# Linear attention with a gated MLP: output weights kept by head group, packed through DRAM for later tiles, and a reordered middle

## The chip, the cores and the metric

One core of a Trainium2 chip runs the whole program. The time is that of the device in microseconds (us), from launch to the last store; the kernel before takes 190.83 us in the median of three runs (190.46 to 190.95). A core has a matrix engine (TensorE, in the profile PE, its weight loads PEld), a vector engine (VectorE, DVE), an engine for activation functions (ScalarE, ACT), a general one (GpSimd, POOL) and a queue engine (SyncE, SP) that here only issues transfers. Each works through its own list of instructions in order and waits on semaphores for the others.

## The reference

A pre-norm block on 2048 rows of 448 columns in bfloat16: linear attention with 16 heads of 28 columns, and a gated MLP of width 1792. Cut to what matters:

```python
phi = lambda t: jnp.where(t > 0, t + 1, jnp.exp(t)) + 1e-6
pq, pk = phi(q), phi(k)
kv = jnp.einsum("bhsd,bhse->bhde", pk, v)
z = jnp.einsum("bhsd->bhd", pk)
num = jnp.einsum("bhqd,bhde->bhqe", pq, kv)
den = jnp.einsum("bhqd,bhd->bhq", pq, z)[..., None] + 1e-6
h = x + (num / den).reshape(B, S, D) @ wo
h2 = h + (gelu(g) * u) @ w_down        # g, u = layernorm(h) @ w_gate, w_up
```

## The kernel before

**Tiles.** The 2048 rows are 16 tiles of 128 rows, or 8 pairs (pair p holds tiles 2p and 2p + 1). Stage A1 normalises each tile, projects it to keys and queries (tasks `k_t`, `q_t`: four matmuls of 448 columns each), applies phi, and sums pk with the normalised x over all tiles (`pt`). From that sum `kv` makes the per-head products; the masked copy of it, `kvm`, multiplied by the output weights, gives `w2`: the attention's output is then pq, divided by its denominator, times w2.

**Stage A2**, one pair at a time (`a2_pair`): `cq` and `aq` finish phi of the queries; `t1` multiplies by z, `dr` sums over the 28 columns of a head, `de` adds epsilon on ScalarE, `rd` takes the reciprocal and `pn` scales pq (into `pqn`). This is transposed, for pair 0 on TensorE (`tro`, evicted by `evo`), for the others by a DMA transpose (`oT_p`, line 605). `out` multiplies by w2, `hr` adds x, `bnst2` and `bnag2` are the statistics of the second layer norm, POOL or ScalarE make its factor, `nh` scales, `wrap` or `wr64` repeats columns, and `trh` (pair 0) or a DMA transpose `hT_t` turns the tile for the MLP. A name ending in P works on a whole pair at once.

**Stage B**: `gu2_v` (chunks of two tiles, v = 0 to 13) and `gu4_v` (four tiles) compute gate and up products into two PSUM banks each, `ge` the gelu on ScalarE, `hm` the product on VectorE, each in two halves of 256 columns; `downA_p` and `downB_p` multiply by w_down for a pair, `fo` adds, `do` stores. wd_sb, the down weights, is loaded by one transfer, `dwd` (line 609), before which `downA_0` can't start.

**How w2 is held before.** Its 448 rows stand in four blocks of 128 rows (the last one overlapping), so that pairs 1 to 7 can run as two matmuls at once, one on the upper 64 rows of the array for one tile and one on the lower 64 for the other (`outA_p`, `outB_p`, lines 627 and 628; seven such steps in all, and `outB_p` waits for `outA_p`, because both add into the same banks). To get the blocks, `kvm` is written with wide zero gaps and `w2` takes seven matmuls (line 547). The other arrangement of the rows, shifted by 64, is made by two transfers from SBUF to SBUF, `dws0` and `dws1`.

**Order.** The order on each engine is written out by hand: `ORDERS` holds one list of task numbers per engine, a task's number being its place in the program. From the dependences `plan` works out which semaphore waits are needed. `HOLD` names, for a task with several waits, the one to issue first (lines 198 to 201).

The orders in the middle, by name (before):

```
PE   pt3_13 pt3_14 pt3_15 q_5 q_4 kv q_7 q_8 w2_2 w2_0 w2_1 q_9 w2_3 tro_1 tro_0 q_6 out1_1 out1_0 q_10 q_11 q_13 q_12
     q_14 q_15 trh_1 trh_0 outA_1 outB_1 gu2_0 gu2_1 outA_2 gu2_2 gu2_3 outB_2 gu2_4 gu2_5 outA_3 gu2_6 outB_3 downA_0 gu2_8 gu2_7
DVE  aq_3 cq_1 evpD_3 z0 aq_1 t1d_0 dr_0 evpD_2 rd_0 dr_1 dr_2 kvm rd_2 kvd dr_3 rd_1 pn_0 rd_3 pn_1 evwD_1 cqP_2 evwD_3
     pn_2 pn_3 aqP_2 hr_1 hr_0 bnst2_1 bnst2_0 bnag2_1 bnag2_0 drP_2 nhD_1 nhD_0 rdP_2 wr64_1 wr64_0 pnP_2 cqP_3 aqP_3 evhD_1
     hr_2 hr_3 bnst2_2 drP_3 hm1_0 hm0_0 bnst2_3 hm0_1 rdP_3 hm1_1 pnP_3
SP   dwg0 dwu0 dwg1 dwu1 dws0 dws1 oT_1 oT_2 dwd oT_3 hT_3 hT_2 hT_4 oT_4 hT_5 hT_7 hT_6 oT_5
```

Of the kernel before, what the change touches and what calls it, by code (L numbers as in the profile page):

```python
# [228 lines left out]
def bass_sequential_preLN__linear_attn_block__glu_gated_geglu__prompt_kernel(  # L229
# [19 lines left out]
    with es:  # L249
# [281 lines left out]
        op("dve", lambda e: e.tensor_tensor(kvz[:, 0:5 * D].rearrange("p (g c) -> p g c", g=NG)[:, :, 0:GW].rearrange("p g (h f) -> p g h f", h=4),  # L531
                                            ps[0:GW, BK_KV, 0:D].rearrange("p (g h f) -> p g h f", g=NG, h=4),
                                            mask[:, :].unsqueeze(1).unsqueeze(3).to_broadcast([GW, NG, 4, DH]), ALU.mult),
           [b_ps[BK_KV], b_mask, b_kvm], [b_kvm], "kvm")
        b_kvd = _Buf("kvd")
        op("dve", lambda e: e.tensor_copy(kvz[:, 4 * D:4 * D + 64], kvz[:, 4 * D - 64:4 * D]), [b_kvm], [b_kvd], "kvd")

        def kvc(g, c):
            o = g * D + c * 128 if c < 3 else 4 * D - 64
            return kvz[:, o:o + 128]  # L540

        for c in range(4):
            def fw2(e, c=c):
                gs = (c, c + 1) if c < 3 else (3,)
                ins = None
                for g in gs:
                    ins = e.matmul(ps[:, BK_W2[c], 0:D], kvc(g, c), wo_sb[:, g, :], start=(g == gs[0]), stop=(g == gs[-1]))  # L547
                return ins
            G.add("pe", fw2, r=[b_kvm, b_wo] + ([b_kvd] if c == 3 else []), w=[b_ps[BK_W2[c]]], name="w2_%d" % c)
            if c % 2 == 0:  # L550
                op("act", lambda e, c=c: e.activation(w2[:, c, :], ps[:, BK_W2[c], 0:D], AF.Identity), [b_ps[BK_W2[c]]], [b_w2[c]], "evwA_%d" % c)
            else:
                op("dve", lambda e, c=c: e.tensor_copy(w2[:, c, :], ps[:, BK_W2[c], 0:D]), [b_ps[BK_W2[c]]], [b_w2[c]], "evwD_%d" % c)
# [4 lines left out]
        def a2_pair(p):
            a = 2 * p
            i2 = p % 2  # L560
            pst = D if p else 512
            if p < 2:
# [7 lines left out]
                for t in (a, a + 1):  # L570
                    n, i = t % 2, t % 4
                    op("dve", lambda e, n=n, i=i: e.tensor_reduce(den[:, i, :], t1[:, n, :].rearrange("p (h d) -> p h d", h=H), AX.X, ALU.add),  # L572
                       [b_t1[n]], [b_den[i]], "dr_%d" % t)
                    op("act", lambda e, i=i: e.activation(den[:, i, :], den[:, i, :], AF.Identity, bias=eps_d[:, 0:1]), [b_den[i], b_epsd], [b_den[i]], "deA_%d" % t)
                    op("dve", lambda e, i=i: e.reciprocal(rd[:, i, :], den[:, i, :]), [b_den[i]], [b_rd[i]], "rd_%d" % t)
                    op("dve", lambda e, t=t, n=n, i=i, i2=i2: e.tensor_tensor(
                        pqn[:, i2, n * pst:n * pst + D].rearrange("p (h d) -> p h d", h=H), pq[:, t, :].rearrange("p (h d) -> p h d", h=H),
                        rd[:, i, :].unsqueeze(2).to_broadcast([128, H, DH]), ALU.mult),
                       [b_pq[t], b_rd[i]], [b_pqn[i2][n]], "pn_%d" % t)
# [243 lines left out]
```

## Time and profile before

| | |
|---|---|
| median of 3 runs | 190.83 us (190.46 to 190.95) |
| span of the profiled execution | 188.3 us |
| TensorE matmul busy | 184.3 us (98%) |
| VectorE busy | 129.3 us (69%) |
| ScalarE busy | 76.5 us (41%) |
| POOL busy | 50.0 us (27%) |

The profile is one execution. Its views: the page (busy shares, the chain of work that ended last, groups of instructions), groups by line and shape, the timeline, which gives the start and the duration of each instruction, and windows, which give busy time for a stretch. A group's row has the line, the engine, the operation, what is written from what, the shapes, the count, then busy us and mean ns, then idle time before. Task names are not in the profile; they follow from the order of each engine's instructions.

### The profile page before, as it was taken

The page shows a single profiled execution, that of the slowest core. Times are in us where ns is not written, and L with a number is a line of the kernel's source. Part 1 is how long each engine was busy: PE and PEld are TensorE (multiplying, and loading weights), DVE is VectorE, ACT ScalarE, POOL GpSimd, SP SyncE. Part 2 cuts the span into 40 slices and gives each one's busy share as a digit, 9 for nine tenths or more (in the row PEclk, how much of TensorE's full clock was granted, in tenths as well). Part 3 has the DMA queues.
Part 4 walks back from the last instruction along what each step waited for, and adds up shares of the span by engine and source line. Part 5 has one row for each costly group of instructions (what it writes and reads, how often), then busy time and mean ns, then how long its engine had stood idle before and what let it go on. Part 6 is the DMA issues. An engine that isn't in the chain of part 4 may idle for free.

```text
span 188.3 us, 4459 instructions
## 1 busy us (share of the span) xinstructions
PE 184.3 (98%) x1813; PEld 109.2 (58%) x1813; DVE 129.3 (69%) x330; ACT 76.5 (41%) x220; POOL 50.0 (27%) x91
## 2 busy tenths in 40 slices
PE   7999999999999999999999999999999999999994
PEld 7545555555688788965554555555545545454554
DVE  4999959999899998786796762562645244335432
ACT  3878752799963231432234222321242222224100
POOL 6067910704505686033614000206100000000000
PEclk9999999999999999999999999999999999999999
DMA  5996458999393526820005720000096000002024
GB/s 169 387 231 88 96 104 194 218 222 174 65 320 64 95 52 116 84 52 0 0 3 98 144 54 0 0 3 2 3 135 111 3 0 24 3 0 98 3 79 140
DMA packets 35076, 17.11 MB, mean 91 GB/s; under 512 B 26864, under 2 KB 33648, under 8 KB 35056
## 3 DMA queue, kind: packets, MB, share of 16 engines
q1 hardware_dynamic: 34432, 16.32, 41.1%
q10 hardware_dynamic: 624, 0.52, 0.8%
q8 instruction: 14, 0.23, 0.5%
q14 instruction: 6, 0.05, 0.1%
HBM read 8.26 MB, written 1.84 MB: 54 GB/s over the span
## 4 chain that ended last, share of the span: by engine, by line
PE 94%; DVE 3%; DMA 1%; issue 0%
PE ps L733 38%; PE ps L697 19%; PE ps L469 12%; PE ps L731 9%; PE ps L488 6%; PE ps L627 3%; PE ps L678 3%; PE ps L628 2%; DMA x_sb<-in_A_x_dram 1%; DVE st L413 1%; PE ps L617 1%; PE ps L547 1%; PE ps L527 1%; PE ps L443 0%; PE ps L654 0%; DVE den L572 0%
## 5 line engine op out<-in xcount | busy, mean ns | idle before, releaser
L733 PE MATMUL ps<-hnT,wgu_sb 64*128 64x512 bf16 (+1 forms) x490 | 88.8, 333 | 0.0
L731 PE MATMUL ps<-hnT,wgu_sb 64*128 64x512 bf16 (+1 forms) x490 | 88.6, 333 | 0.0
L751 ACT ACTIVATE gl<-ps 128x256 bf16<-128x256 f32 x112 | 36.6, 383 | 85.3 <-PE ps L731 84.4
L753 DVE TENSOR_TENSOR hh<-ps,gl 128x256 bf16<-128x256 f32 x112 | 42.1, 416 | 41.4 <-ACT gl L751 41.3
L733 PEld LDWEIGHTS ps<-hnT,wgu_sb 64*128 64x128 bf16 x490 | 45.2, 94 | 32.9 <-DVE hh L753 3.4
L731 PEld LDWEIGHTS ps<-hnT,wgu_sb 64*128 64x128 bf16 x490 | 45.4, 94 | 2.5
L697 PE MATMUL ps<-wd_sb,hh 64*128 64x448 bf16 x392 | 41.5, 349 | 0.0
L697 PEld LDWEIGHTS ps<-wd_sb,hh 64*128 64x128 bf16 x392 | 23.2, 94 | 14.5
L469 PE MATMUL ps<-wqk_sb,xnT 128*128 128x448 bf16 x128 | 27.4, 353 | 0.0
L413 DVE BATCH_NORM_STATS2 st<-x_sb 128x6 f32<-128x448 bf16 x32 | 19.2, 612 | 1.8 <-DMA x_sb<-in_A_x_dram 1.7
L585 POOL TENSOR_TENSOR t<-pq,zbc 128x448 f32<-128x448 bf16 x12 | 12.3, 1042 | 23.7 <-DVE pq L583 22.0
L469 PEld LDWEIGHTS ps<-wqk_sb,xnT 128*128 128x128 bf16 x128 | 11.9, 98 | 11.4 <-DVE pk L482 0.8
L488 PE MATMUL ps<-pk,xnn 128*128 128x448 bf16 x64 | 13.9, 352 | 0.0
L627 PE MATMUL ps<-w,pqnT 64*128 64x448 bf16 x49 | 11.5, 349 | 0.1
L425 POOL TENSOR_SCALAR ln<-mv 128x2 f32<-128x2 f32 x7 | 2.0, 291 | 35.2 <-DVE mv L414 35.0
L480 ACT ACTIVATE e<-ps 128x448 bf16<-128x448 f32 x16 | 8.5, 539 | 5.6 <-PE ps L469 5.5
L628 PE MATMUL ps<-pt_sb,pqnT 64*128 64x448 bf16 x42 | 10.2, 350 | 0.0
L633 DVE TENSOR_TENSOR x_sb<-ps,x_sb 128x448 bf16<-128x448 f32 x16 | 9.6, 616 | 0.7 <-PE ps L628 0.6
L662 POOL TENSOR_SCALAR hn<-x_sb,nm,rs 128x448 bf16<-128x448 bf16 x14 | 9.9, 719 | 0.4
L482 DVE SCALAR_TENSOR_TENSOR pk<-ps,e 128x448 bf16<-128x448 f32 x16 | 9.8, 617 | 0.1
L488 PEld LDWEIGHTS ps<-pk,xnn 128*128 128x128 bf16 x64 | 6.3, 98 | 5.9 <-DVE pk L482 0.3
L453 POOL TENSOR_SCALAR xnn<-x_sb,nm,rs 128x448 bf16<-128x448 bf16 x12 | 8.9, 744 | 2.2 <-ACT rs L422 1.9
(85 smaller groups left out, 160.5 us busy)
## 6 DMA issues: line engine op xcount, KB each, us to landing
out_dram<-x_sb SPq DMA_DIRECT2D x15, 112.0 KB, 1.8
wd_sb<-in_B_w_down_dram SPq DMA_DIRECT2D x1, 1568.0 KB, 8.4
x_sb<-in_A_x_dram SPq DMA_DIRECT2D x3, 448.0 KB, 5.9
wgu_sb<-in_B_w_gate_dram SPq DMA_DIRECT2D x1, 896.0 KB, 12.1
wgu_sb<-in_B_w_up_dram SPq DMA_DIRECT2D x1, 896.0 KB, 16.5
wgu_sb<-in_B_w_gate_dram SPq DMA_DIRECT2D x1, 672.0 KB, 6.1
wgu_sb<-in_B_w_up_dram SPq DMA_DIRECT2D x1, 672.0 KB, 8.5
wo_sb<-in_A_wo_dram SPq DMA_DIRECT2D x1, 392.0 KB, 7.5
```

What stands on the lines that cost most here:

```text
L413: op("dve", lambda e: e.bn_stats(st[:, t, :], src_ap), [b_src], [b_st[t]], "bnst%s_%d" % (tag, t))
L469: ins = e.matmul(ps[:, bk, 0:D], xnT[:, t, k, :], wqk_sb[:, k, c0:c0 + D], start=(k == 0), stop=(k == 3))
L488: ins = e.matmul(ps[:, BK_PT[c], 0:D], xnn[:, t % XN_R, c * 128:(c + 1) * 128], pk[:, ip, :], start=(t == 0), stop=(t == T - 1))
L585: op("pool", lambda e, n=n: e.tensor_tensor(t1[:, n, :], pq[:, a + n, :], zbc[:, :], ALU.mult), [b_pq[a + n]] + b_z, [b_t1[n]], "t1p_%d" % ...
L627: e.matmul(ps[:, BK_OUT[0], 0:D], pqnT[ra, i2, sg // 2, :], w2[ra, sg // 2, :], start=(sg == 0), stop=(sg == 5))
L628: ins = e.matmul(ps[:, BK_OUT[1], 0:D], pqnT[rb, i2, 3 + (sg + 1) // 2, :], (w2 if sg == 6 else w2s)[rb, sg // 2, :], start=(sg == 0), sto ...
L662: op("pool", lambda e, t=t, sh=sh: e.tensor_scalar(hn[:, sh, 0:D], x_sb[:, t, :], nm2[:, t:t + 1], rs2[:, t:t + 1], ALU.add, ALU.mult), [b ...
L697: ins = e.matmul(ps[:, bko[half][n], 0:D], hh[rows, j, sl[n]], wd_sb[rows, j, :], start=(j == 0 and (half == 0 or p == 6)), stop=(j == NJ ...
L731: first = e.matmul(psG[:, jj * N:(jj + 1) * N], wgu_sb[A_, k, j * 128:(j + 1) * 128], hnT[A_, ka_, c0:c0 + N], start=(k == 0), stop=(k == ...
L733: ins = e.matmul(psU[:, jj * N:(jj + 1) * N], wgu_sb[B_, k, j * 128:(j + 1) * 128], hnT[B_, kb_, c0:c0 + N], start=(k == 0), stop=(k == NK ...
L751: G.add("act", lambda e, gi=gi, cs_=cs_, psG=psG: e.activation(gl[:, gi, cs_], psG[:, cs_], AF.Gelu_apprx_tanh), r=[b_ps[BK_G[i]]], w=[b_g ...
L753: op("dve", lambda e, dst=dst, srcU=srcU, srcL=srcL: e.tensor_tensor(dst, srcU, srcL, ALU.mult), [b_ps[BK_U[i]], b_glh], [b_ar[j_][t % HR] ...
```

## The change

- **Output weights by head group.** `kvm` is written without gaps; `w2` takes four matmuls, one per group of four heads (112 rows), evicted into `w2g`. Pairs 0 and 1 now both use `w2g` with four full matmuls per tile (`out1_t`); pair 1's queries are scaled into four blocks of 128 columns, so its DMA transpose moves 1024 columns, not 896. `kvd` is gone.
- **Packed for later pairs through DRAM.** `dw2w` writes `w2g` to a DRAM tensor; when that has landed, `dw2r0` and `dw2r1` read it back in blocks of 64 rows, to the upper and to the lower half of `w2p`, which takes the place of pt_sb and wv_sb. Pairs 2 to 7 (`outA`, `outB`) use `w2p`. `dws0` and `dws1` are gone.
- **Epsilon as a 29th column.** `t1` has 29 columns a head, the last one set to epsilon once; `dr` sums 29 columns, and the ten additions on ScalarE (`deA`, `deP`) are gone.
- **Whole-bank gate products.** In the chunks of two tiles `ge` and `hm` are one instruction of 512 columns each (`geW`, `hmW`), not two of 256.
- **Orders.** From `pt3_13` to about `gu4_14` the five lists differ; ahead and behind they are the same, apart from the pads on POOL. `HOLD` now names a wait for nearly every task from the first to the last.

The orders in the middle (after):

```
PE   pt3_13 q_4 pt3_14 pt3_15 q_7 q_5 kv q_9 w2_2 w2_0 w2_1 q_6 w2_3 tro_1 tro_0 q_11 q_8 out1_0 out1_1 q_10 q_13 q_15 q_12
     q_14 trh_0 trh_1 out1_2 out1_3 gu2_0 gu2_1 gu2_2 outA_2 gu2_3 outB_2 gu2_4 outA_3 gu2_5 outB_3 gu2_6 downA_0 gu2_7 gu2_8
DVE  aq_3 cq_1 aq_1 z0 t1d_0 dr_0 evpD_3 evpD_2 rd_0 dr_1 rd_1 dr_2 kvm pn_1 pn_0 evwD_1 dr_3 rd_2 rd_3 evwD_3 cqP_2 pn_2
     aqP_2 pn_3 hr_0 hr_1 bnst2_0 bnst2_1 bnag2_0 cqP_3 bnag2_1 drP_2 nhD_0 nhD_1 wr64_0 cqP_4 wr64_1 rdP_2 aqP_3 cqP_6 evhD_1
     pnP_2 hr_2 hr_3 drP_3 hmW_0 rdP_3 pnP_3 hmW_1 aqP_4 bnst2_3 hmW_2 bnag2_3 bnst2_2
SP   dwg0 dwu0 dwg1 dwu1 dw2w oT_1 dw2r0 dw2r1 oT_2 oT_3 dwd hT_3 hT_2 oT_4 hT_5 hT_4 hT_6 hT_7 oT_5
```

The core of the diff:

```diff
-        wv_sb = sb("wv_sb", [128, 4, D], BF16)
+        pv_sb = sb("pv_sb", [128, 8, D], BF16)
+        pt_sb, wv_sb, w2p = pv_sb[:, 0:4, :], pv_sb[:, 4:8, :], pv_sb[:, 0:NK, :]
...
-        w2 = sb("w2", [128, 4, D], BF16)
-        t1 = sb("t1", [128, 2, D], F32)
+        w2g = sb("w2g", [GW, NG, D], BF16)
+        w2d = nc.dram_tensor("w2_bounce", [D, D], BF16)
+        t1 = sb("t1", [128, 2, H, DH + 1], F32)
...
-        op("pool", lambda e: e.memset(eps_d[:], EPS), [], [b_epsd], "epsd")
+        op("pool", lambda e: e.memset(t1[:, :, :, DH:DH + 1], EPS), [], [b_epsd], "epsd")
...
-        op("pool", lambda e: e.memset(kvz[:, GW:15 * GW], 0.0), [], [b_kvm], "kvzpad")
+        for i_ in range(2):
+            op("pool", lambda e, i_=i_: e.memset(pqn[:, i_, :].rearrange("p (n g c) -> p n g c", n=2, g=NG)[:, :, :, GW:128], 0.0), [], b_pqn[i_], "pqnpad_%d" % i_)
...
+        for g in range(NG):
+            G.add("pe", lambda e, g=g: e.matmul(ps[0:GW, BK_W2[g], 0:D], kvz[:, g * GW:(g + 1) * GW], wo_sb[:, g, :], start=True, stop=True),
+                  r=[b_kvm, b_wo], w=[b_ps[BK_W2[g]]], name="w2_%d" % g)
...
-        for h, (to, of) in enumerate(((A_, B_), (B_, A_))):
-            dma("sp", w2s[to, :, :], w2[of, 0:3, :], [b_w2s[h]], "dws%d" % h, r=b_w2[0:3], after=xts[-1:])
+        dma("sp", w2d.ap().rearrange("(g p) n -> p g n", p=GW), w2g[:, :, :], [b_w2d], "dw2w", r=b_w2, after=xts[-1:])
+        for h, rows in enumerate((A_, B_)):
+            dma("sp", w2p[rows, :, :], w2d.ap().rearrange("(k p) n -> p k n", p=64), [b_w2p[h]], "dw2r%d" % h, r=[b_w2d])
...
-                    op("act", lambda e, i=i: e.activation(den[:, i, :], den[:, i, :], AF.Identity, bias=eps_d[:, 0:1]), [b_den[i], b_epsd], [b_den[i]], "deA_%d" % t)
...
-                G.add("sp", lambda e, i2=i2: e.dma_start_transpose(pqnT[:, i2, 0:NK, :], pqn[:, i2, 0:2 * D]),
+                G.add("sp", lambda e, i2=i2: e.dma_start_transpose(pqnT[:, i2, 0:8 if p == 1 else NK, :], pqn[:, i2, 0:1024 if p == 1 else 2 * D]),
...
-            if p == 0:
+            if p < 2:
                 for n in range(2):
                     def fout(e, W, n=n):
...
-                            ins = e.matmul(ps[:, BK_OUT[n], 0:D], pqnT[:, i2, 4 * n + g, :], w2[:, g, :], start=(g == 0), stop=(g == NG - 1))
+                            ins = e.matmul(ps[:, BK_OUT[n], 0:D], pqnT[0:GW, i2, 4 * n + g, :], w2g[:, g, :], start=(g == 0), stop=(g == NG - 1))
...
-                for hh_ in range(2):
-                    cs_ = slice(hh_ * 256, (hh_ + 1) * 256)
+                for hh_ in range(2 if nj == 1 else 1):
+                    cs_ = slice(hh_ * 256, (hh_ + 1) * 256) if nj == 1 else slice(0, 512)
```

More of the change, by code (lines that the diff above doesn't have):

```diff
@@ L297, in bass_sequential_preLN__linear_attn_block__glu_gated_geglu__prompt_kernel @@
         gl = sb("gl", [128, 3, 512], BF16)
-        kvz = hh[0:GW, 6:9, :].rearrange("p a b -> p (a b)")
-        w2s = pt_sb[:, 0:3, :]
+        t1f = t1[:].rearrange("p n h d -> p n (h d)")[:, :, 0:D]
+        kvz = hh[0:GW, 6, 0:D]
         ps = es.enter_context(nc.psum_tensor("ps", [128, 8, 512], F32))
@@ L320, in bass_sequential_preLN__linear_attn_block__glu_gated_geglu__prompt_kernel @@
         b_eq, b_pq = bufs("eq", T), bufs("pq", T)
-        b_pt, b_z, b_kvm, b_w2, b_w2s = bufs("pt", 4), bufs("z", 2), _Buf("kvm"), bufs("w2", NG), bufs("w2s", 2)
+        b_pt, b_z, b_kvm, b_w2, b_w2d, b_w2p = bufs("pt", 4), bufs("z", 2), _Buf("kvm"), bufs("w2", NG), _Buf("w2d"), bufs("w2p", 2)
         b_t1, b_den, b_rd = bufs("t1", 2), bufs("den", 4), bufs("rd", 4)
@@ L533, in bass_sequential_preLN__linear_attn_block__glu_gated_geglu__prompt_kernel @@
                                             mask[:, :].unsqueeze(1).unsqueeze(3).to_broadcast([GW, NG, 4, DH]), ALU.mult),
[L534 to L551, printed above, removed]
-            else:
-                op("dve", lambda e, c=c: e.tensor_copy(w2[:, c, :], ps[:, BK_W2[c], 0:D]), [b_ps[BK_W2[c]]], [b_w2[c]], "evwD_%d" % c)
@@ L560, in a2_pair @@
             i2 = p % 2
-            pst = D if p else 512
             if p < 2:
@@ L626, in foutp @@
                             ra, rb = (A_, B_) if sg % 2 == 0 else (B_, A_)
-                            e.matmul(ps[:, BK_OUT[0], 0:D], pqnT[ra, i2, sg // 2, :], w2[ra, sg // 2, :], start=(sg == 0), stop=(sg == 5))
-                            ins = e.matmul(ps[:, BK_OUT[1], 0:D], pqnT[rb, i2, 3 + (sg + 1) // 2, :], (w2 if sg == 6 else w2s)[rb, sg // 2, :], start=(sg == 0), stop=(sg == 5))
+                            e.matmul(ps[:, BK_OUT[0], 0:D], pqnT[ra, i2, sg // 2, :], w2p[ra, sg, :], start=(sg == 0), stop=(sg == 5))
+                            ins = e.matmul(ps[:, BK_OUT[1], 0:D], pqnT[rb, i2, 3 + (sg + 1) // 2, :], w2p[rb, sg, :], start=(sg == 0), stop=(sg == 5))
                         return ins
-                    parts.append(G.add("pe", foutp, r=b_pqnT[i2] + b_w2 + b_w2s, w=[b_ps[b_] for b_ in BK_OUT], name="out%s_%d" % (part, p), sync=parts[-1:]))
+                    parts.append(G.add("pe", foutp, r=b_pqnT[i2] + b_w2p, w=[b_ps[b_] for b_ in BK_OUT], name="out%s_%d" % (part, p), sync=parts[-1:]))
             for t in (a, a + 1):
@@ L749, in gu_chunk @@
                         srcL = gl[:, gi, cs_].rearrange("p (a n) -> p a n", a=njh)
-                    b_glh = b_gl2[gi][hh_]
+                    b_glh = b_gl2[gi][hh_:] if nj > 1 else b_gl2[gi][hh_:hh_ + 1]
                     G.add("act", lambda e, gi=gi, cs_=cs_, psG=psG: e.activation(gl[:, gi, cs_], psG[:, cs_], AF.Gelu_apprx_tanh),
-                          r=[b_ps[BK_G[i]]], w=[b_glh], name="ge%d_%d" % (hh_, v), after=[tbl2])
+                          r=[b_ps[BK_G[i]]], w=b_glh, name="ge%s%d_%d" % ("W" if nj > 1 else "", hh_, v), after=[tbl2])
                     op("dve", lambda e, dst=dst, srcU=srcU, srcL=srcL: e.tensor_tensor(dst, srcU, srcL, ALU.mult),
-                       [b_ps[BK_U[i]], b_glh], [b_ar[j_][t % HR] for j_ in jr for t in th], "hm%d_%d" % (hh_, v))
+                       [b_ps[BK_U[i]]] + b_glh, [b_ar[j_][t % HR] for j_ in jr for t in th], "hm%s%d_%d" % ("W" if nj > 1 else "", hh_, v))
         done, t0, tbl2 = 0, 0, None
```

38 lines of the change are left out of this document (18 added, 20 removed), and 133 rows, old and new, of tables (HOLD, ORDERS).

## The prediction

> **What bounds the kernel now.** First the page: its busy shares and the chain that ended last.
>
> ```profile
> span 188.3 us, 4459 instructions
> PE 184.3 (98%) x1813; PEld 109.2 (58%) x1813; DVE 129.3 (69%) x330; ACT 76.5 (41%) x220; POOL 50.0 (27%) x91
> PE 94%; DVE 3%; DMA 1%; issue 0%
> ```
>
> TensorE issues almost without a break, and the chain is TensorE for 94%. So an edit pays only if it takes matmul slots away or closes one of the few holes, and it costs only where it opens a hole. The profiled span is 188.3 us; the median of the runs is 190.83 us, so what lies around the span is 2.5 us, which I leave as it is. Next I read the timeline of TensorE in the middle, where the change sits:
>
> ```profile
> 34.23 1.68 PE L469 MATMUL ps<-wqk_sb,xnT 128*128 128x448 bf16 x8
> 35.96 1.03 PE L527 MATMUL ps<-pt_sb,wv_sb 128*112 128x112 bf16 x16
> 36.83 1.68 PE L469 MATMUL ps<-wqk_sb,xnT 128*128 128x448 bf16 x8
> ...
> 48.95 0.35 PE L627 MATMUL ps<-w,pqnT 64*128 64x448 bf16 x1
> ...
> 49.14 0.35 PE L627 MATMUL ps<-w,pqnT 64*128 64x448 bf16 x1
> ...
> 49.56 0.36 PE L627 MATMUL ps<-w,pqnT 64*128 64x448 bf16 x1
> ...
> 63.49 0.57 PE L697 MATMUL ps<-wd_sb,hh 64*128 64x448 bf16 x4
> ```
>
> A 448-column matmul takes a slot of 0.19 us (48.95 to 49.14; its 0.35 is latency). Two holes show. Eight matmuls from 34.23 need 1.5 us, yet kv starts at 35.96: 0.23 lost, waiting for the last eviction of pt_sb. And outB_1 starts 0.42 after the last step of outA_1, not 0.19: 0.23 lost, since outB_1 waits for outA_1 to drain. The last row is downA_0, the first matmul that reads wd_sb; all of gu2_0 to gu2_6 and pairs 2 and 3 of the output projection precede it in both orders. I use its start, 63.49, as the gauge.
>
> **The change, part by part.** *Output weights by group.* w2 goes from seven matmuls to four: 3 x 0.19 = 0.57 saved. Pair 1 of the output projection goes from seven two-row-group slots to eight full ones: 0.19 lost, and the drain of 0.23 goes with it. kvd disappears; kvm still feeds w2.
>
> *A projection moved forward.* q_4 slips in between pt3_13 and pt3_14, so twelve matmuls from 34.23, not eight, lie ahead of kv: it starts at 34.23 + 12 x 0.188 = 36.5, by when the evictions are in. The 0.23 hole closes.
>
> *Epsilon column, whole-bank gate products.* For these the VectorE groups of the stretch from kvm to pnP_3 matter (window 37.19 to 56.25), and the two ends of it:
>
> ```profile
> L413 DVE BATCH_NORM_STATS2 st<-x_sb 128x6 f32<-128x448 bf16 x4 | 2.4, 614 | 0.0
> L633 DVE TENSOR_TENSOR x_sb<-ps,x_sb 128x448 bf16<-128x448 f32 x4 | 2.4, 619 | 0.6 <-PE ps L628 0.6
> L576 DVE TENSOR_TENSOR pqn<-pq,rd 128x448 bf16<-128x448 bf16 x4 | 2.3, 588 | 0.0
> L590 DVE TENSOR_TENSOR pqn<-pq,rd 128x896 bf16<-128x896 bf16 x2 | 2.2, 1086 | 0.0
> L586 DVE TENSOR_REDUCE den<-t 128x32 f32<-128x896 f32 x2 | 2.1, 1060 | 0.0
> L753 DVE TENSOR_TENSOR hh<-ps,gl 128x256 bf16<-128x256 f32 x4 | 1.5, 403 | 0.1
> L583 DVE TENSOR_TENSOR pq<-pq,eq 128x896 bf16<-128x896 bf16 x2 | 1.2, 622 | 0.0
> L553 DVE CAST w<-ps 128x448 bf16<-128x448 f32 x2 | 1.2, 617 | 0.0
> L572 DVE TENSOR_REDUCE den<-t 128x16 f32<-128x448 f32 x2 | 1.2, 615 | 0.1
> L582 DVE TENSOR_SCALAR eq<-eq 128x896 bf16<-128x896 bf16 x3 | 1.2, 385 | 0.0
> L575 DVE RECIPROCAL rd<-den 128x16 f32<-128x16 f32 x3 | 0.7, 241 | 0.0
> L589 DVE RECIPROCAL rd<-den 128x32 f32<-128x32 f32 x2 | 0.7, 348 | 0.0
> L645 DVE TENSOR_SCALAR hn<-x_sb,mv,rs 128x448 bf16<-128x448 bf16 x2 | 0.7, 388 | 0.0
> L660 DVE COPY hnT<-ps 128x896 bf16<-128x896 bf16 x1 | 0.6, 620 | 0.0
> L531 DVE TENSOR_TENSOR hh<-ps,mask 112x448 bf16<-112x448 f32 x1 | 0.6, 614 | 0.0
> L414 DVE BATCH_NORM_AGGREGATE mv<-st 128x2 f32<-128x6 f32 x2 | 0.3, 172 | 0.0
> L647 DVE COPY hn<-hn 128x64 bf16<-128x64 bf16 x2 | 0.2, 142 | 0.0
> L536 DVE COPY hh<-hh 112x64 bf16<-112x64 bf16 x1 | 0.1, 140 | 0.0
> ```
>
> ```profile
> 37.19 0.61 DVE L531 TENSOR_TENSOR hh<-ps,mask 112x448 bf16<-112x448 f32 x1
> ...
> 55.17 1.08 DVE L590 TENSOR_TENSOR pqn<-pq,rd 128x896 bf16<-128x896 bf16 x1
> ```
>
> Idle time is 0.8 us in 19: in the middle VectorE, not TensorE, sets when things get ready. The window's edges catch one op more at each end (a 16-column reduce, cqP_4); without these it holds 41 ops of 21.25 us in 19.06 us. With the idle (0.65 us that the rows name, 0.8 in all) neighbours overlap by 2.84 to 3.0 us over 40 joints: 0.075 us each.
>
> The new ops have no row. The whole-bank product: 0.403 below (it can't be cheaper than half of itself), 0.806 above (two halves); a 448-column read of PSUM takes 0.617 and a 256-column one 0.403, so 1.1 ns a column: 0.68. A reduce over 29 columns: 1.060 below, 1.060 x 29/28 = 1.10 above; I take 1.10. For the gelu and the removed additions:
>
> ```profile
> L751 ACT ACTIVATE gl<-ps 128x256 bf16<-128x256 f32 x6 | 2.0, 381 | 1.7 <-PE ps L731 1.6
> ...
> L574 ACT ACTIVATE den<-den,eps_d 128x16 f32<-128x16 f32 x4 | 1.2, 310 | 0.1
> L602 ACT ACTIVATE pqnT<-ps 128x512 bf16<-128x512 bf16 x2 | 1.1, 598 | 0.0
> ```
>
> A 512-column gelu is bounded by 0.38 and 0.76; I take 0.60 from the 512-column row. The additions of epsilon leave ScalarE 0.31 each, hidden behind projections, but take a round trip out of each den to rd to pn chain. T1's rows of 29 columns may slow POOL's products: below nothing, above half of their time again; the first reader of the pairs (drP_3) has about 0.7 us of room, so I take nothing. The two pads in place of pqnpad and the missing kvzpad lie in the first microseconds, where TensorE waits for the first layer norm on VectorE and ScalarE: nothing, either way. HOLD only puts one wait of several first: at most one more wait instruction ahead of an op, hidden where the op isn't late, and inside the bounds below where it is.
>
> *VectorE's new chain.* From kvm to pnP_3 the new order has 36 ops: kvm, 4 pn, dr_3, 2 rd, 2 evwD, 4 cqP (2, 3, 4, 6), 2 aqP, 4 hr, 2 bnst2 and 2 bnag2, drP_2, drP_3, 2 nhD, 2 wr64, rdP_2, rdP_3, evhD_1, one hmW, 2 pnP. By the rows 19.5 us; less 35 x 0.075, 16.85 us. Four hm shrink to one, two bnst2 move behind pnP_3, two cqP move ahead of it. kvm starts when kv ends, 36.5 + 1.03 = 37.55. So pnP_3 ends at about 54.4, where before it ended at 56.25.
>
> *What TensorE meets.* w2_2 waits for kvm: kv (0.87 from 35.96 to 36.83) and q_9 (0.75) leave TensorE free at 38.1, kvm ends at 38.2: 0.1. trh_0 waits for wr64_0, the 23rd op of the same chain: 11.5 - 22 x 0.075 = 9.9 after 37.55, at 47.4, while TensorE, now ahead, comes at 47.0: 0.4. gu2_2 wants its bank back from hmW_0, the 34th, which ends at 53.1; TensorE is there at 47.4 + 0.75 (two trh) + 1.5 (eight matmuls) + 3.05 (gu2_0 and gu2_1, 28 pairs of 256 columns) = 52.7: 0.4. Each of the three is 0 at the least and twice that at the most. Sum for the gauge: 63.49 - 0.57 + 0.19 - 0.23 - 0.23 + 0.1 + 0.4 + 0.4 = 63.55. So the matmuls saved are given back to VectorE, and the local edits come out even, if nothing else is late.
>
> *Queue of SP.* What else is late is wd_sb. Before, dwd stood directly behind oT_2; now SP issues dw2w, oT_1, dw2r0, dw2r1, oT_2, oT_3, dwd, so dwd waits behind oT_3, that is for pnP_3.
>
> ```profile
> 48.30 1.23 SPq L605 DMA_TRANSPOSE pqnT<-pqn  x1
> 49.57 0.59 SPq L346 DMA_DIRECT2D wd_sb<-in_B_w_down_dram  x1
> ```
>
> ```profile
> 49.50:51.30 1.80, 1.74 (x28) 1.35 (x30) 1.22 (x3) 1.78 (x5) 1.80 (x2) 1.00 0.87 142
> 51.30:56.30 5.00, 5.00 (x90) 4.21 (x88) 4.91 (x11) 3.34 (x8) 0.59 (x2) 1.00 0.96 308
> ```
>
> ```profile
> wd_sb<-in_B_w_down_dram SPq DMA_DIRECT2D x1, 1568.0 KB, 8.4
> ...
> pt_sb<-w SPq DMA_DIRECT2D x2, 168.0 KB, 5.7
> hnT<-hn SPq DMA_TRANSPOSE x14, 3.0
> ```
>
> The transpose occupies SP for 1.23 us, then dwd goes out and lands 8.4 us later, at 57.9: 5.5 us ahead of downA_0. The windows (their last two columns: DMA share and GB/s) say how the 8.4 us are made up: until 51.3 the engines still work on the transpose, 1.5 MB move by 56.3, and the rest is stragglers. In the new order the same pair goes out later: oT_3 at 54.4, dwd 1.27 behind it at 55.7, landed at 64.1. TensorE is there at 63.55. So downA_0 starts at about 64.15, 0.65 behind before. Bounds of the landing: 6.7 us after issue without stragglers (62.4), 10.1 with twice their 1.7 us (65.8); I take 8.4, since the same transpose goes ahead of it.
>
> The Trainium skill, page DMA: Bandwidth & Descriptors, section "Anatomy of one DMA — SWDGE (gpsimd) path", fits 2.0 us + bytes/436 GB/s to a DMA; for 1.6 MB that would be an estimated 5.7 us, dwd would land at 61.4 and hold nothing up. The trace's 8.4 us for this very load disagrees, and the load goes out by another path than the fit's.
>
> The detour through DRAM: dw2r0 waits on SP for dw2w to land, and oT_2, oT_3, dwd and the hT transposes are queued behind it. Its bounds are the landing of the old shifted copies, 5.7 us behind the gate and up loads, and twice that; issued at 41.1 it is there by 47 to 52.5, while oT_2 isn't wanted before 50.3, and w2p not before outA_2 at 54.5. I take nothing, 1 us at the far end. Behind dwd come hT_3 and hT_2, issued at about 61 and wanted by gu2_7 2.6 us after downA_0 starts; a transpose takes SP 1.23 us and lands after 3.0, and two in flight share that, so 1.23 to 1.5 each behind the load: 0 to 0.4 more, I take 0.
>
> **The rivals.** The forecast: wd_sb is late, downA_0 starts 0.65 late, and no later stage gives it back, since TensorE is full to the end. 190.83 + 0.65 = 191.5.
>
> Rival 1, not slower: wd_sb is in time. One mechanism: the 8.4 us were the transpose in flight ahead of it and stragglers; if the load takes under 7.8 us from 55.7, downA_0 starts at 63.55, and the time is 190.83 + 0.06 = 190.9. For it: between 51.3 and 56.3 the engines moved 308 GB/s, at which 1568 KB take 5.2 us. Against it: it will again go out 1.27 us behind a transpose.
>
> Rival 2, faster outright: wd_sb in time and none of the three new waits for VectorE there (0.9), because its chain is shorter than I make it: 190.83 - 0.84 = 190.0. Against it: the chain is VectorE's throughput, and TensorE runs ahead of it.
>
> Rival 3, more than the forecast: the hT_3 and hT_2 transposes, queued behind a late wd_sb, hold gu2_7 as well, or the bounce holds SP and so oT_3 and dwd: another 0.5 to 1, about 192.3.
>
> **How the numbers follow.** Forecast 0.52, rival 1 0.17, rival 2 0.13, rival 3 0.18. Forecast's own range: 190.9 to 192.1. The range reaches from rival 2's near side to rival 3: 190.2 to 192.6; the far bound of the landing (193.2) is left out. A difference that can be told from none is 0.3%, 0.57 us; the forecast stands just beyond it. Slower: 0.6 of the forecast and all of rival 3, 0.50. Faster: most of rival 2 and a little of rival 1, 0.15. The rest, 0.35, is the same.
>
> **What would show it.** Right: TensorE waits 0.4 to 0.9 us ahead of the first matmul of downA_0, for the DMA into wd_sb; dwd issued at about 55.7; pnP_3 ends at about 54.4; trh_0 waits for VectorE; no 0.23 hole within pair 1 and none ahead of kv. Wrong: dwd landed before 63 and downA_0 started before 63.5; or the hole lies elsewhere, ahead of outA_2 (then the bounce) or of gu2_7 (then the transposes).

## The result and the profile after

The changed kernel takes 191.69 us (191.34 to 192.08, seven runs), the kernel before 190.83 beside it (190.40 to 191.26, seven runs): ratio 1.0052, 95% interval 1.0035 to 1.0069, so 0.67 to 1.32 us longer. The prediction said 191.5. The page of the changed kernel, first its span, busy shares and chain:

```profile
span 189.9 us, 4403 instructions
PE 184.6 (97%) x1804; PEld 110.9 (58%) x1804; DVE 130.2 (69%) x315; ACT 73.1 (39%) x196; POOL 49.0 (26%) x91
PE 79%; DVE 12%; DMA 6%; SPq 1%; ACT 0%; issue 0%; DVEq 0%
```

TensorE's busy time is about that of before (184.3), but the chain that ended last now runs 12% through VectorE and 6% through transfers, where it was 3% and 1%: TensorE waits for others in places. Two views say where. First the timeline of TensorE ahead of the middle, before and after (start, duration, instruction, in brackets idle time and its releaser):

```profile
31.96 0.73 PE L488 MATMUL ps<-pk,xnn 128*128 128x448 bf16 x3
```

```profile
15.53 0.92 PE L540 MATMUL ps<-wqk_sb,xnT 128*128 128x448 bf16 x4 [0.60 <-DMA xnT<-xnn]
...
32.99 0.73 PE L559 MATMUL ps<-pk,xnn 128*128 128x448 bf16 x3
```

The third matmul of the last row is pt1_15, the last one ahead of the stretch that the change reorders; it starts at 32.34 before and at 33.37 after. So 1.03 us is lost in a part where TensorE's order is the same in both: 0.76 of it ahead of k_4 (15.53), which waits for the transpose xT_4, and most of the rest ahead of that. Everything of the middle is therefore compared as time behind pt1_15. Now the timeline of TensorE in the middle of the changed kernel:

```profile
47.68 0.54 PE L540 MATMUL ps<-wqk_sb,xnT 128*128 128x448 bf16 x2
48.37 0.34 PE L712 MATMUL ps<-ident,hn 128*128 128x128 bf16 x3
...
54.32 0.28 PE L791 MATMUL ps<-hnT,wgu_sb 64*128 64x256 bf16 x1 [0.22 <-DVE hh L811]
...
55.76 0.35 PE L685 MATMUL ps<-pv_sb,pqnT 64*128 64x448 bf16 x1
...
63.00 0.27 PE L789 MATMUL ps<-hnT,wgu_sb 64*128 64x256 bf16 x1
63.47 0.28 PE L791 MATMUL ps<-hnT,wgu_sb 64*128 64x256 bf16 x1 [0.20 <-DVE hh L811]
...
64.90 0.54 PE L755 MATMUL ps<-wd_sb,hh 64*128 64x448 bf16 x3
...
67.63 0.28 PE L789 MATMUL ps<-hnT,wgu_sb 64*128 64x256 bf16 x1
```

The holes: 0.31 ahead of trh_0 (the last projection's second matmul starts at 47.87, its slot ends at 48.06); 0.4 inside gu2_2 (54.32, its bank comes back from hmW_0); 0.4 inside gu2_6 (63.00 to 63.47, the next matmul of such a pair follows 0.1 behind otherwise; hmW_4). The brackets show less, because a matmul in flight counts as busy. Ahead of downA_0 (64.90) there is no hole. SP's timeline and the landing of wd_sb:

```profile
51.61 5.30 SPq L663 DMA_TRANSPOSE pqnT<-pqn  x2
56.95 0.58 SPq L417 DMA_DIRECT2D wd_sb<-in_B_w_down_dram  x1
62.84 3.04 SPq L723 DMA_TRANSPOSE hnT<-hn  x2
```

```profile
wd_sb<-in_B_w_down_dram SPq DMA_DIRECT2D x1, 1568.0 KB, 7.4
```

dwd goes out at 56.95 and lands at 64.3, 0.6 us ahead of downA_0. So the wait on which the prediction rested is not in this profile. VectorE's and POOL's timelines around the holes:

```profile
50.18 1.40 DVE L648 TENSOR_TENSOR pqn<-pq,rd 128x896 bf16<-128x896 bf16 x1
...
53.59 0.67 DVE L811 TENSOR_TENSOR hh<-ps,gl 128x512 bf16<-128x512 f32 x1
...
54.56 1.09 DVE L648 TENSOR_TENSOR pqn<-pq,rd 128x896 bf16<-128x896 bf16 x1
...
61.71 1.10 DVE L722 COPY hn<-hn 128x448 bf16<-128x448 bf16 x1 [0.50 <-POOL hn L720]
62.73 0.68 DVE L811 TENSOR_TENSOR hh<-ps,gl 128x512 bf16<-128x512 f32 x1
63.33 0.26 DVE L722 COPY hn<-hn 128x448 bf16<-128x448 bf16 x1
```

```profile
49.52 2.97 POOL L644 TENSOR_TENSOR t<-pq,zbc 128x448 f32<-128x448 bf16 x2 [3.63 <-DVE pq L642]
...
61.64 1.04 POOL L644 TENSOR_TENSOR t<-pq,zbc 128x448 f32<-128x448 bf16 x1
```

The same column copy takes 0.26 us (wrap_2) and 1.10 (wrap_3); the long one lies over POOL's product t1p_9 (61.64 to 62.68). hmW_4 (62.73) stands behind it, and gu2_6 waits for hmW_4. Likewise pnP takes 1.09 alone (54.56) and 1.40 over a POOL product (50.18). The Trainium skill, page SBUF — State Buffer, section "Who interferes with whom", says that VectorE and GpSimd share a pair of SBUF ports, held for a whole instruction, and that a copy in a two-port mode, or an operation with two SBUF inputs beside a GpSimd read, waits for it. The trace agrees: the long copy ends 0.13 behind the POOL product. The kernel before has such a copy too, where TensorE does not wait for it: wrap_7 took 1.03 us and ended 0.13 behind a product (72.47 to 73.51).

### The profile page after: what moved, and what is told of

Its sections match the earlier page's. It is cut to its first block, busy times and chain, and to the rows that moved or that the text cites. A ratio compares the mean times of both kernels' runs of the same rounds, so it can differ in the third digit from the quotient of the medians.

```text
span 189.9 us, 4403 instructions
## 1 busy us (share of the span) xinstructions
PE 184.6 (97%) x1804; PEld 110.9 (58%) x1804; DVE 130.2 (69%) x315; ACT 73.1 (39%) x196; POOL 49.0 (26%) x91
## 4 chain that ended last, share of the span: by engine, by line
PE 79%; DVE 12%; DMA 6%; SPq 1%; ACT 0%; issue 0%; DVEq 0%
PE ps L791 34%; PE ps L755 19%; PE ps L789 10%; PE ps L540 5%; PE ps L559 4%; DMA x_sb<-in_A_x_dram 3%; PE ps L736 3%; DMA xnT<-xnn 3%; PE ps L685 2%; PE ps L686 2%; DVE den L631 1%; DVE st L484 1%; DVE pqn L635 1%; DVE den L645 1%; DVE x_sb L691 1%; DVE pqn L648 1%
## 5 line engine op out<-in xcount | busy, mean ns | idle before, releaser
L809 ACT ACTIVATE gl<-ps 128x256 bf16<-128x256 f32 (+1 forms) x98 | 35.5, 414 | 89.4 <-PE ps L789 88.4
L811 DVE TENSOR_TENSOR hh<-ps,gl 128x256 bf16<-128x256 f32 (+1 forms) x98 | 41.1, 455 | 41.4 <-ACT gl L809 41.2
L755 PEld LDWEIGHTS ps<-wd_sb,hh 64*128 64x128 bf16 x392 | 24.2, 94 | 13.3
L644 POOL TENSOR_TENSOR t<-pq,zbc 128x448 f32<-128x448 bf16 x12 | 13.6, 1143 | 24.9 <-DVE pq L642 23.4
L685 PE MATMUL ps<-pv_sb,pqnT 64*128 64x448 bf16 x42 | 9.9, 349 | 0.0
L686 PE MATMUL ps<-pv_sb,pqnT 64*128 64x448 bf16 x42 | 9.9, 349 | 0.0
```

The source lines that it names most:

```text
L644: op("pool", lambda e, n=n: e.tensor_tensor(t1[:, n, :, 0:DH], pq[:, a + n, :].rearrange("p (h d) -> p h d", h=H), zbc[:, :].rearrange("p ...
L685: e.matmul(ps[:, BK_OUT[0], 0:D], pqnT[ra, i2, sg // 2, :], w2p[ra, sg, :], start=(sg == 0), stop=(sg == 5))
L686: ins = e.matmul(ps[:, BK_OUT[1], 0:D], pqnT[rb, i2, 3 + (sg + 1) // 2, :], w2p[rb, sg, :], start=(sg == 0), stop=(sg == 5))
L755: ins = e.matmul(ps[:, bko[half][n], 0:D], hh[rows, j, sl[n]], wd_sb[rows, j, :], start=(j == 0 and (half == 0 or p == 6)), stop=(j == NJ ...
L809: G.add("act", lambda e, gi=gi, cs_=cs_, psG=psG: e.activation(gl[:, gi, cs_], psG[:, cs_], AF.Gelu_apprx_tanh), r=[b_ps[BK_G[i]]], w=b_gl ...
L811: op("dve", lambda e, dst=dst, srcU=srcU, srcL=srcL: e.tensor_tensor(dst, srcU, srcL, ALU.mult), [b_ps[BK_U[i]]] + b_glh, [b_ar[j_][t % HR ...
```

## The experiments

The measured times, with where pt1_15 starts in the one profiled execution, and what follows behind it. The first two rows are the two kernels; each ratio is to the kernel before, run beside it on the same chip (190.39 to 190.57 in the median there). The last three columns are from the one profile, with the span read from the trace to 0.01 us. A profile can stand at the end of its kernel's scatter: its span is 192.9 us in b_dwd (190.5 to 192.9 over the runs), 192.2 in a_ve (190.3 to 192.2), 193.6 in a_both (191.1 to 193.8) and 191.5 in a_dwd1 (191.3 to 195.5).

| run | median us | ratio, 95% | pt1_15 | downA_0 behind it | end of span behind it |
|---|---|---|---|---|---|
| before | 190.83 | 1 | 32.34 | 31.15 | 155.92 |
| after | 191.69 | 1.0052 (1.0035 to 1.0069) | 33.37 | 31.53 | 156.56 |
| a_same | 191.73 | 1.0061 (1.0037 to 1.0084) | 33.23 | 31.55 | 156.69 |
| a_nohold | 191.68 | 1.0063 (1.0041 to 1.0085) | 32.99 | 31.55 | 156.69 |
| a_dwd | 193.39 | 1.0148 (1.0120 to 1.0176) | 32.99 | 33.40 | 158.32 |
| b_dwd | 193.03 | 1.0152 (1.0110 to 1.0193) | 32.99 | 33.47 | 159.93 |
| a_ve | 193.09 | 1.0129 (1.0109 to 1.0148) | 33.28 | 33.96 | 158.88 |
| a_dwd1 | 195.83 | 1.0237 (1.0191 to 1.0282) | 32.67 | 33.93 | 158.85 |
| a_both | 193.93 | 1.0205 (1.0162 to 1.0248) | 32.61 | 36.00 | 160.95 |
| b_whole | 190.77 | 1.0010 (0.9997 to 1.0023) | 33.10 | 31.15 | 155.94 |
| a_split | 191.27 | 1.0032 (1.0021 to 1.0043) | 32.93 | 31.53 | 156.45 |
| a_lean | 190.97 | 1.0011 (0.9999 to 1.0023) | 32.66 | 31.45 | 156.21 |
| a_best | 191.59 | 1.0053 (1.0038 to 1.0068) | 32.76 | 32.15 | 156.93 |
| a_free | 190.73 | 1.0011 (0.9994 to 1.0028) | 32.79 | 30.63 | 155.41 |

Two theories went in. VectorE: the middle is set by VectorE's chain, which gives the saved matmuls back in waits. wd_sb (the prediction's): the late load holds downA_0. The rival to both was that the loss lies in the early part, as the one profile had it.

**a_same: the changed kernel again.**

> The changed kernel again, as it is. In the profile shown, downA_0 starts 1.41 us later than before, and 1.03 of that is already there when pt1_15 starts, since the transposed load of xT_4 landed at 15.39 us, not 13.56. Theory early: this is the change's own doing; xT_4 lands after 15 us again and the span is 1.5 us over that of the kernel before. Rival chance: the early loads land now so, now so, in any kernel; here xT_4 lands before 14.5 us or the kernel before shows the same scatter, and the part lost behind pt1_15 stays near 0.4. Both expect a ratio near 1.005.

The rival, chance, came true: xT_4 landed at 13.81 us, so it does not always land late. But pt1_15 is late all the same (33.23): TensorE lost the time in other waits, the longest 0.5 ahead of k_6 (18.37). So xT_4 alone does not make the early loss. Over all profiles it lands at 13.6 to 14.0 or at 15.0 to 15.4: late in after, a_dwd, a_ve and a_split, early in the other kernels made from after. Of the three that share the early program of before it landed at 13.56 (before), 13.98 (b_dwd) and 15.19 (b_whole). pt1_15 starts anywhere from 32.34 to 33.10 there, and from 32.61 to 33.37 in the kernels made from after. The early part thus scatters by 0.8 us in either family, while what follows pt1_15 repeats: downA_0 31.53 and 31.55 behind it, against 31.15. It repeats although the waits ahead of it do not: in a_same outA_2 starts 0.2 later (55.83), held by oT_2, which landed at 55.78, and the wait for hmW_4 then takes that in, so downA_0 comes out the same. A difference of some tenths between the means of the two families can't be excluded with three profiles on one side; the section on the prediction estimates it from the spans of all runs.

**a_nohold: no order of waits given.**

```diff
-HOLD = {
-    20: (19,), 32: (31,), 34: (33,), 35: (34,), 37: (34,), 41: (40,), 43: (42,), 44: (43,), 46: (43,),
...
-}
+HOLD = {}
```

> The changed kernel with no entry in HOLD, so that of several waits always the youngest ticket is issued first. Theory of the prediction: HOLD is worth nothing either way, time within 0.3 us of the changed kernel. Rival early: the entries for the early tasks delay the first microseconds, and without them pt1_15 starts up to 1.0 us earlier and the time is about 190.7.

191.68 us against the 191.73 of a_same: HOLD is worth nothing, and it is not the cause of the early loss (pt1_15 at 32.99).

**a_dwd and b_dwd: the load's place on SP.**

```diff
 a_dwd (from after)
-SP ... dw2r1 oT_2 oT_3 dwd hT_3
+SP ... dw2r1 oT_2 dwd oT_3 hT_3
 b_dwd (from before)
-SP ... oT_1 oT_2 dwd oT_3 hT_3
+SP ... oT_1 oT_2 oT_3 dwd hT_3
```

> The changed kernel with dwd directly behind oT_2 on SP, as it was before, so that it no longer waits for pnP_3. Theory wd_sb: in most runs downA_0 is held by wd_sb, and with dwd issued at about 53 us and landed by 61.5 the time falls by 0.3 to 0.65, to about 191.1. Rival early plus VectorE: wd_sb is there 0.57 us ahead of downA_0 in the profile shown, the loss lies ahead of it, and the time stays within 0.15 of the changed kernel. Third possibility: oT_3 and the hT transposes now go out into a running 1568 KB load and land later, and the time grows by some tenths.

> The kernel before with only dwd moved behind oT_3 on SP. pnP_3 ends at 56.25 there, so dwd goes out at about 57.5 and by 7.4 to 8.4 us lands at 64.9 to 65.9, while downA_0 wants it at 63.49. Theory wd_sb: slower by 1.4 to 2.4 us, all of it a wait ahead of downA_0, with nothing given back behind. Rival: the load shrinks to the 5.2 us that 308 GB/s would make of it, lands at 62.7, and the time does not change.

a_dwd is the third possibility, and far dearer than some tenths. Its timeline of SP, and of TensorE at outA_3:

```profile
53.45 0.59 SPq L389 DMA_DIRECT2D wd_sb<-in_B_w_down_dram  x1
55.30 2.63 SPq L635 DMA_TRANSPOSE pqnT<-pqn  x1
```

```profile
62.01 0.35 PE L657 MATMUL ps<-pv_sb,pqnT 64*128 64x448 bf16 x1 [1.99 <-DMA pqnT<-pqn]
```

oT_3, issued 1.85 us behind the load, landed at 61.87, after the load (60.99): 6.6 us instead of 2.9. outA_3 waits 2 us for it. So the place behind oT_3 that the changed kernel gives to dwd is the better one for its order. In before, oT_3 goes out (56.28) only 1.65 ahead of the load's landing, and the question does not arise.

b_dwd is slower, as theory wd_sb said: dwd went out at 58.20 and landed at 66.33, and downA_0 waited until 66.46, 2.32 later behind pt1_15 than before. "With nothing given back behind" holds as well; more was lost, which the last section shows.

**a_ve: VectorE's order mended; a_dwd1: the load earlier still; a_both.**

```diff
 a_ve
-DVE bnag2_1 drP_2 nhD_0 nhD_1 wr64_0 cqP_4 wr64_1 rdP_2 aqP_3 cqP_6 evhD_1 pnP_2 hr_2 hr_3 drP_3 hmW_0 rdP_3 pnP_3 hmW_1 aqP_4 ... wrap_3 hmW_4
+DVE bnag2_1 cqP_4 nhD_0 wr64_0 nhD_1 wr64_1 drP_2 aqP_3 rdP_2 evhD_1 pnP_2 hr_2 hr_3 aqP_4 hmW_0 drP_3 rdP_3 pnP_3 cqP_6 hmW_1 ... hmW_4 wrap_3
 a_dwd1
-SP ... dw2w oT_1 dw2r0 dw2r1 oT_2 oT_3 dwd hT_3
+SP ... dw2w oT_1 dwd dw2r0 dw2r1 oT_2 oT_3 hT_3
```

> The changed kernel with VectorE's order mended alone: drP_2 behind wr64_1, aqP_4 and hmW_0 ahead of drP_3, cqP_6 behind pnP_3, hmW_4 ahead of wrap_3. Theory VectorE: the three waits of TensorE for it (0.3 ahead of trh_0, 0.4 ahead of outA_2, 0.4 ahead of the second half of gu2_6) close, TensorE is ready for downA_0 1.1 us earlier; but pnP_3 ends 0.6 later, so dwd goes out at about 57.5 and lands at 64.5 to 65, and now TensorE does wait for wd_sb ahead of downA_0, 0.6 to 1.2 us. Nearly all is given back: time 0 to 0.3 below the changed kernel. Rival: the holes come from something else (PSUM banks, ScalarE) and stay, time the same or up to 0.6 longer.

> The changed kernel with dwd directly behind oT_1 on SP, ahead of the two read-backs and of oT_2. The load goes out at about 45.3 and wd_sb is there by 54, but the read-backs (wanted by outA_2 at 55.8) and oT_2 (the same) are queued behind 1568 KB. Theory VectorE: wd_sb was not what held downA_0 in the runs so far, so nothing is gained, and the time is the same if the read-backs and oT_2 land before 55.8. Rival contention: they land after it, by what the load takes (oT_2 landed 3.6 us behind its issue; 6.6 us were seen of oT_3 behind a running load): up to 2 us longer.

> The changed kernel with both: VectorE's order mended, dwd directly behind oT_1. Theory VectorE and wd_sb as two bounds close together: only with both moved does the time fall, by 0.7 to 1.1 us, to 190.6 to 191.0, about that of the kernel before. Rival contention: outA_2 waits for the read-backs or for oT_2, and the time is above 191.7.

a_ve was meant to close holes and lost 1.4 us in the median. VectorE's, POOL's and SP's timelines of it, the landing of wd_sb, and TensorE inside gu2_3:

```profile
55.06 0.35 DVE L619 RECIPROCAL rd<-den 128x32 f32<-128x32 f32 x1
55.44 1.65 DVE L620 TENSOR_TENSOR pqn<-pq,rd 128x896 bf16<-128x896 bf16 x1
57.01 0.38 DVE L613 TENSOR_SCALAR eq<-eq 128x896 bf16<-128x896 bf16 x1
```

```profile
55.10 1.04 POOL L616 TENSOR_TENSOR t<-pq,zbc 128x448 f32<-128x448 bf16 x1 [1.86 <-DVE den L617]
```

```profile
57.12 1.22 SPq L635 DMA_TRANSPOSE pqnT<-pqn  x1
58.38 0.58 SPq L389 DMA_DIRECT2D wd_sb<-in_B_w_down_dram  x1
```

```profile
wd_sb<-in_B_w_down_dram SPq DMA_DIRECT2D x1, 1568.0 KB, 8.7
```

```profile
58.05 0.28 PE L763 MATMUL ps<-hnT,wgu_sb 64*128 64x256 bf16 x1 [1.54 <-DVE hh L783]
```

The hole ahead of trh_0 did close (trh_0 14.69 behind pt1_15, after 15.00). But aqP_4, moved ahead, released POOL's t1p_8 at 55.10, just ahead of pnP_3, which then took 1.65 instead of 1.09. pnP_3 ended at 57.09, 1.5 later than in after, and two things stand behind it. On VectorE it is hmW_1: it ended at 57.99, and gu2_3, which wants its bank back, waited 1.6 us for it (58.05). On SP it is the prediction's chain: oT_3, dwd 58.38, landed 67.11, and downA_0 waited another 1.1 us, until 67.24. So pnP_3 can set downA_0 through two transfers in a row, once it is late by more than half a microsecond, but here the longer wait was VectorE's. This profile is the longest execution of a_ve, so its sizes are those of that one.

a_dwd1 and a_both went the rival's way: with 1568 KB ahead of them in the queue, dw2r1 landed at 57.03 and 57.58, oT_2 at 57.78 and 58.32, and outA_2 started at 57.83 and 58.36 (55.76 in after). In a_dwd1:

```profile
57.83 0.36 PE L657 MATMUL ps<-pv_sb,pqnT 64*128 64x448 bf16 x1 [2.51 <-DMA pqnT<-pqn]
```

**b_whole: the whole-bank products alone, in the kernel before.**

```diff
-                for hh_ in range(2):
+                for hh_ in range(2 if nj == 1 else 1):
...
-                    b_glh = b_gl2[gi][hh_]
+                    b_glh = b_gl2[gi][hh_:] if nj > 1 else b_gl2[gi][hh_:hh_ + 1]
```

> The kernel before with the whole-bank gate products alone, each in the place of the later of its two halves. Theory of the prediction: VectorE saves 0.13 us for each of the 14, TensorE is the bound, so time within 0.3 us of the kernel before. Rival: a bank comes back later, since the product now waits for the whole gelu (0.60 + 0.68 against 0.38 + two halves of 0.40 in step), and gu2 steps wait in the middle: up to 1 us longer.

downA_0 stands 31.15 behind pt1_15, exactly as in before, and the ratio's interval holds 1: this part alone changes nothing. The epsilon column and the new w2 were not tried alone, as each needs orders of its own.

**a_split, a_lean, a_best: the bounds taken away one by one.**

```diff
 a_split
-dma("sp", wd_sb[:, :, :], ..., [b_wd], "dwd", after=[G.all[-1]])
+for h_ in range(2):
+    G.add("sp", lambda e, js=slice(7 * h_, 7 * h_ + 7): e.dma_start(wd_sb[:, js, :], ...),
+          w=[b_wd[h_]], name="dwd%d" % h_, kind="dma")
+SP ... oT_2 dwd0 oT_3 dwd1 hT_3
 a_lean
-DVE ... cqP_2 ... cqP_3 ... cqP_4 ... cqP_6
+DVE ... (the four left out)
 a_best (a_split, and)
+DVE bnag2_1 cqP_4 nhD_0 wr64_0 nhD_1 wr64_1 drP_2 evhD_1 aqP_3 rdP_2 pnP_2 hr_2 hr_3 hmW_0 drP_3 rdP_3 pnP_3 hmW_1 ... hmW_2 ... cqP_6 hr_5
+ACT ... geW_4 wrap_2 wrap_3 geW_5
+SP ... hT_2 hT_3
```

> The changed kernel with the load of wd_sb in two halves of 784 KB, the first directly behind oT_2, the second behind oT_3. Theory VectorE: downA_0 is not held by wd_sb as the kernel stands, so nothing is gained at it; hT_3 and hT_2 no longer run beside a load and land 0.5 us earlier, which takes away the wait of some 0.1 us ahead of gu2_7: time 0 to 0.2 below the changed kernel. Rival wd_sb: 0.5 or more below it. Rival contention: oT_3 lands behind the first half, after 60 us, outA_3 waits, and the time grows.

> The changed kernel without cqP_2, cqP_3, cqP_4 and cqP_6: the clamp of the queries' exponential at 1 and its epsilon are left out for tiles 4 to 9, 12 and 13, so VectorE does four ops of 0.38 us less, two ahead of wr64_0 and all ahead of pnP_3; TensorE's work, the transfers and the orders stay. Theory VectorE: wr64_0 is 0.6 us earlier, pnP_3 1.2 us; the waits ahead of trh_0 (0.3) and of outA_2 (most of 0.4) go, wd_sb is no bound, and the time falls by 0.6 to 1.0, to about 190.9. Rival: TensorE's holes have another cause, and the time falls by less than 0.3.

> The changed kernel with what the runs so far point to: the load of wd_sb in two halves; drP_2 and then evhD_1 behind wr64_1; hmW_0 ahead of drP_3; cqP_6 behind hmW_2; the column copies wrap_2 and wrap_3 on ScalarE, which is idle there, in the place of VectorE, and hT_2 ahead of hT_3. aqP_4 stays where it was, so that POOL's product of tile 8 does not meet pnP_3. Theory VectorE: the waits ahead of trh_0, outA_2, in gu2_6 and ahead of gu2_7 go (0.3, 0.3, 0.4, 0.1), pnP_3 ends some 0.4 later with no harm, as wd_sb is half there; 190.6 to 190.9, about the kernel before. Rival: each wait closed opens the next one, and the time stays within 0.3 of the changed kernel.

a_split: downA_0 does not move (31.53). Behind it 0.1 is gained: hT_2 landed at 66.64, no longer beside a load, and gu2_7 need not wait. wd_sb does not hold the changed kernel as it stands. The median is 0.42 below that of after, on another chip, and the two intervals overlap; what of it is more than this 0.1 stays open.

a_lean leaves out clamps that the result needs, so it is no kernel to use, but it tells the two theories' shares. Behind pt1_15, trh_0 comes 0.23 earlier and outA_2 0.49 earlier than in after: these waits were VectorE's. Then most is given back. Its TensorE and SP at downA_0, and the load's landing:

```profile
64.11 0.36 PE L654 MATMUL ps<-wd_sb,hh 64*128 64x448 bf16 x2 [0.17 <-DMA wd_sb<-in_B_w_down_dram]
```

```profile
54.44 1.22 SPq L562 DMA_TRANSPOSE pqnT<-pqn  x1
55.70 0.59 SPq L315 DMA_DIRECT2D wd_sb<-in_B_w_down_dram  x1
```

```profile
wd_sb<-in_B_w_down_dram SPq DMA_DIRECT2D x1, 1568.0 KB, 8.3
```

Here downA_0 does wait for wd_sb: dwd 55.70, landed 63.98, the matmul at 64.11, with a hole of 0.3 ahead of it (the last pair of gu2_6 starts at 63.67 and has a slot of 0.11). The expectation "wd_sb is no bound" was wrong. The median fell by 0.7 against after, but only 0.35 of it stands behind pt1_15 in the profiles; the rest can't be told from the scatter of the early part. So the time that was expected came out, but not for the reason given.

a_best failed: its pnP_2 again met POOL's products.

```profile
50.04 1.77 DVE L546 TENSOR_TENSOR pqn<-pq,rd 128x896 bf16<-128x896 bf16 x1
...
54.92 1.09 DVE L546 TENSOR_TENSOR pqn<-pq,rd 128x896 bf16<-128x896 bf16 x1
```

1.77 us where it takes 1.09 alone, and three waits stand behind it: gu2_2 0.4 for hmW_0 (53.53), outA_2 0.2 for oT_2, which landed at 55.30 (55.35), and gu2_3 0.4 for hmW_1 (56.67). The waits ahead of trh_0, in gu2_6 and ahead of gu2_7 did close. Each wait closed opened the next one, as its rival had it.

**a_free: all bounds at once.**

```diff
 a_split + the wraps on ACT of a_best + the four clamps left out of a_lean
```

> Three things at once: the four clamps left out as in a_lean (the queries' exponential of tiles 4 to 9, 12 and 13 goes unclamped and without its epsilon), the load of wd_sb in two halves as in a_split, and the column copies wrap_2 and wrap_3 on ScalarE with hT_2 ahead of hT_3 as in a_best. Theory of bounds one behind the other: in a_lean the waits ahead of trh_0 and outA_2 are gone, but 0.4 us in gu2_6 for hmW_4 and 0.4 ahead of downA_0 for wd_sb (landed at 63.98) took their place; with both of these closed too, downA_0 starts at most 30.75 us behind pt1_15 (a_lean 31.45, the kernel before 31.15), so that the 0.4 to 0.8 us that TensorE saves show at last: 190.0 to 190.4, at or below the kernel before. Rival: oT_3 behind the first half, or oT_2, opens another wait, downA_0 stays 31.2 us or more behind pt1_15, and the time is 190.7 or more.

```profile
63.42 0.35 PE L659 MATMUL ps<-wd_sb,hh 64*128 64x448 bf16 x1
```

downA_0 at 63.42 is 30.63 behind pt1_15, 0.52 less than before and 0.90 less than after, and the whole span behind pt1_15 is 0.51 below that of before. No hole over 0.12 is left between pt1_15 and downA_0. So the matmuls saved are real, and behind pt1_15 they show once VectorE, the load and the transposes are all out of the way. It is no even comparison, though: a_free, like a_lean, leaves out clamps on VectorE that before still has. And the median (190.73, ratio 0.9994 to 1.0028) still does not fall below before: the expected 190.0 to 190.4 was missed. The spans of its runs go from 188.2 to 189.6, those of before beside it from 188.3 to 189.2; the profiled one is the shortest. No version tried beats the kernel before.

## Why the prediction was right, and where it was not

- *TensorE is the bound, the saved matmuls come back as waits:* right. Behind pt1_15, tro_0 stands 0.67 ahead of before (the terms up to there gave 0.57 + 0.23 - 0.1 = 0.70), gu2_0 0.40 (0.34).
- *The new waits for VectorE:* right in place and near in size. Ahead of w2_2 0.12 (predicted 0.1), ahead of trh_0 0.31 (0.4), for hmW_0 0.4 (0.4). pnP_3 ended at 55.65, that is 54.6 less the 1.03 of the early part (54.4); the chain took 17.10 us from kvm's start, not 16.85, and pnP_2 alone lost 0.3 beside POOL's products. The whole-bank product took 0.68, the 29-column reduce 1.10, the 512-column gelu 0.60, as taken.
- *POOL's products no slower:* right for the products themselves, 1.04 us alone before and after. *Nothing else late up to downA_0:* this step failed. hmW_4 was late by 0.4 behind wrap_3, a copy of 1.10 instead of 0.26 beside a POOL product. Without it the local edits stand even at downA_0 (+0.38 - 0.4), as the prediction had them. With the two copies on ScalarE (a_free) gu2_6 has no such hole.
- *wd_sb late, downA_0 waits 0.65:* this step failed for the kernel as it is, and with it the prediction's own first sign, a wait of 0.4 to 0.9 ahead of downA_0. dwd went out as predicted (56.95 less 1.03 is 55.9, against 55.7) but landed 0.6, 0.5 and 0.9 ahead of downA_0 in after, a_same and a_nohold: the load took 7.0 to 7.4 us, not 8.4. By these numbers it would have been just in time in all three even without the 0.4 for hmW_4. That a later load does hold downA_0 is shown by a_lean, where the load took 8.3 us and the matmul followed its landing by 0.13, and by a_ve and b_dwd.
- *The detour through DRAM, nothing:* the time was right, the size was not. dw2w went out at 42.12 and the second read-back landed at 54.32, 12.2 us later, past the bounds of 5.7 and 11.4. It was there 1.4 ahead of outA_2 (55.76). But oT_2, in flight beside it, took 3.6 us and landed at 55.20, 0.6 ahead of outA_2, and in a_same it held outA_2.
- *The sum:* +0.65 predicted behind an unchanged early part, +0.64 measured there (156.56 against 155.92). That these agree is luck: the 0.6 for wd_sb is not in the profile, and in its place stand 0.4 for hmW_4, 0.1 ahead of gu2_7 and 0.1 among the late gate products (157.72), which the forecast did not have.
- *The early part:* the rest of the 0.86 us lies ahead of pt1_15. The two profiles are 1.60 apart, since before happened to be profiled at the near end of its scatter and after at the far end. The spans of all runs say less: on the chip of a_same and a_nohold their means are 189.62 and 189.63, that of before 188.58. Of these 1.05 us, 0.77 stands behind pt1_15 in the profiles, so by estimate 0.3 is lost ahead of it on average, which the prediction put at nothing. HOLD is not the cause; the pads on POOL, which also differ there, were not tried alone. This and why xT_4 lands at one of two times stay open.
- *Rivals:* rival 1 (wd_sb in time, by a load of under 7.8 us) came true for the load, but not for the time. Rival 3's second half, the transposes behind the load, shows as 0.1 ahead of gu2_7 (67.63, hT_2 landed at 67.59).
